# FNet and routed feed-forward on one core: w_r products read from PSUM, half columns of group two compared on GpSimd

## The chip, the core and the metric

The kernel runs on one core of one Trainium2 chip. The core has five engines with a queue each: TensorE (PE, with its weight loads as PEld), VectorE (DVE), ScalarE (ACT), GpSimd (POOL) and SyncE (SP). SP issues most of the loads, GpSimd issues the indirect loads and the stores. The metric is the device time of one execution in microseconds (us); several executions are timed and their median is given. A profiled execution has a time of its own, and a span: from the first to the last event that the profile shows.

## The reference, cut to what matters

A token sequence x of 2048 x 576 goes through two sublayers. The first normalises it and mixes it by two discrete Fourier transforms of which the real part is kept; the matrices of the transforms are inputs. The second scores each token with w_r, takes the one token with the highest score, runs a gated feed-forward of width 4608 on it, and adds the result to that row alone.

```python
xn = layernorm(x)
a, b = xn @ Wd_re.T, xn @ Wd_im.T
h = x + (Ws_re @ a - Ws_im @ b)
hn = layernorm(h)
r = hn @ w_r
i = argmax(r)                       # one token of 2048
y = (silu(hn[i] @ w_gate) * (hn[i] @ w_up)) @ w_down
out = h + hn                        # and, for row i alone:
out[i] += y * sigmoid(r[i])
```

## The kernel before, in words

The kernel uses symmetries that a matrix of such a transform has (columns that mirror one another, halves that repeat up to a sign), so that it computes with a quarter of each. It does not take them on trust: it loads the whole matrices, compares the parts that should mirror each other on VectorE (`off_s`, `off_t` and `off_h`, lines 375, 380 and 387), and ScalarE squares the differences and sums them up (`square`, line 368). If the sum of all squares is not nearly zero, a general path runs at the end in place of the short one; with these inputs it does not.

The 16 column blocks of the sequence matrices are folded into nine, which are worked on in two groups (`GROUPS`): blocks 1 to 5, and blocks 6, 7, 0 and 8. For each group PE runs the sequence transform (`seq`, line 565, five matmul groups numbered 0 to 4), ScalarE and VectorE bring its sums to Z (`keep`, lines 579 and 583), and PE runs the hidden transform block by block (`hid`, line 610). VectorE adds x to each result (`residual`, line 619) and multiplies the row with w_r and sums it up (`dot_h`, line 623); ScalarE takes the variance (`spread_of`, line 630). From these come the scores (`scores`, lines 639 to 642), in three batches, and the finished rows: 14 blocks on ScalarE (`result`, line 661), two on GpSimd (`result_on_pool`, line 654). GpSimd stores ten of the sixteen blocks (lines 676 and 678), SP the other six (`store_if`, line 1079), either early or as the last thing on its queue, by where the token lies.

The comparison by halves, `off_h`, takes one or two column blocks of a group and one of the two matrices (real, imaginary): two operations, one subtracts and one adds the two halves of 64 columns of every other piece. `c_half` plans them: two operations' worth for the real and two for the imaginary matrix, then one square over both. Group one has three such steps, group two has two (`HALVES`), with two column blocks each. The differences lie in Q, which has two slots; a slot is free again when ScalarE has squared it. The tiles D hold the matrices, D2 and D0 those of group two; once they have been used and compared, weights are loaded into them.

Then the token is found: VectorE takes the maximum of the scores over the columns, PE spreads it over the partitions (`spread`, line 255), VectorE picks row and column (`token`, `where`), ScalarE picks the token's row (`row_of_token`, line 1058), PE spreads it to all partitions (`to_all`, lines 1090 and 1091), VectorE normalises it into PSUM (`normalized`, line 1098), and ScalarE copies it to SBUF for GpSimd (`copy_xs`, line 1103).

The feed-forward runs over 36 rows of weights per partition in nine blocks of four. A block has a tile of w_gate, of w_up and of w_down, each loaded with 1152 KB (`load_ffn`, line 1200; two loads where the place is split, lines 1202 and 1208). There are 16 places for such tiles: in D, in the raw tiles R, in XF, W, Z and Q. The first 16 loads are issued as these come free, Q's last; the others follow when a tile's products are done. The down tiles of the last three blocks come behind all gate and up tiles. Products of gate and up rows with the token's row are taken by VectorE (line 1217, with the sum; line 1224, without) and by GpSimd (line 1228, 14 of them); ScalarE sums up what has no sum (line 1233). Per block ScalarE and VectorE form the gate (lines 1244 to 1247), and PE multiplies with the down tile (`down`, line 1255). Last, VectorE adds to the token's row (line 1268), and ScalarE's queue stores it (line 1278).

PSUM has eight banks. Four are used in pairs under the name y, four one by one under the name z: two for each `seq` group, two for each fold of an even block, and one each for the two spread keys (`pm`), the sum of errors (`pk`), the gate (`hs`), the output row (`pd`) and a matmul that only keeps PE busy (`spin`).

The order of each queue comes from a planner. `add` states an operation with its engine, an estimated duration and what it depends on; `order` computes for each the longest way to the end and then fills each engine's queue in time, taking of the operations that are ready the one with the longest way (`push` adds to it; the products with w_r have a push of -40, so that they come last among what is ready). The planner's times are estimates; at run time each queue runs in that order, and each operation waits for what it needs.

Of the kernel before, what the change touches and what calls it, by code (L numbers as in the profile page):

```python
# [7 lines left out]
F32 = mybir.dt.float32  # L8
# [3 lines left out]
OP = mybir.AluOpType  # L12
AX = mybir.AxisListType

P = 128
# [127 lines left out]
def kernel(  # L143
# [21 lines left out]

    def bank(name, tag, bufs):
        return psum.tile([P, 512], F32, tag=tag, name=name, bufs=bufs)

    def ypair(name):
# [4 lines left out]
    def ybank(name):  # L174
        return ypair(name)[0]

    def zbank(name):
        return bank(name, "z", 4)

# [62 lines left out]
    def newton(rs, sd, var, unit, scale, tag):  # L242
# [7 lines left out]
        dve.scalar_tensor_tensor(rs, u, 1.5 * scale, r0, op0=OP.add, op1=OP.mult)  # L250

    def spread(col, tag):

        pb = zbank(f"pm{tag}")
        pe.matmul(pb[:, :P], col.to_broadcast([P, P]), ident, start=True, stop=True)
        return pb[:, :P]
# [120 lines left out]
    def off_t(j, i, u):  # L377

        o = Q[:, u % 2, 14 * P : QW].rearrange("p (k m) -> p k m", m=P)
        dve.tensor_tensor(o, C[NK - j, i, False], C[j, i, False][:, :, ::-1], op=SIGN[i])  # L380

    def off_h(g, c, n, i, u):

        o = Q[:, u % 2, i * 9 * n * HM : (i + 1) * 9 * n * HM].rearrange("p (c k m) -> p c k m", k=9, m=HM)
        t = DT[g, i][:, c : c + n]
        for k, op in enumerate((OP.subtract, OP.add)):
            dve.tensor_tensor(o[:, :, k::2, :], t[:, :, k::2, 0:HM], t[:, :, k::2, HM:P], op=op)  # L387

# [141 lines left out]
    def fold(k):  # L530
        if k % 2:
            FO[k] = ypair(f"fo{k}")
        else:
            FO[k] = zbank(f"fe{k}"), zbank(f"fo{k}")
        for t, c, w in zip(FO[k], (1, 289), (288, 287)):
# [20 lines left out]
    def seq(g, n):  # L556

        w = len(GROUPS[g]) * HM
        ZP[g, n] = [zbank(f"ps{g}_{n}_{h}") for h in range(2)]
        parts = [(0, E0 + 2 * P, 64, 0), (1, O0 + 2 * P, 64, 64)]  # L560
# [60 lines left out]
    def dot_h(k):  # L621
        n = POS[k]
        dve.scalar_tensor_tensor(  # L623
            junk2, X[:, k, 0:D], 1.0, wr, op0=OP.mult, op1=OP.mult, accum_out=TD[:, n, 0:1]
        )

    def spread_of(k):
# [204 lines left out]
    def c_half(g, c, m):  # L832
        u, w = qs.take()
        cus = [[CU[j, i, False] for j in GROUPS[g][c : c + m]] for i in range(2)]
        n = [
            add("DVE", 0.16 + 0.62 * m, then(off_h, g, c, m, i, u), [d for _, d in cus[i]], w)
            for i in range(2)
        ]
        for i in range(2):
            for b, _ in cus[i]:  # L840
                users[b].append(n[i])
        squares(u, 9 * m * P, n)

    def squares(u, w, n, ps=P):
        SQUARES.append(add("ACT", 0.3 + w / 1200, then(square, u, w, ps), n))
        qs.users[u].append(SQUARES[-1])
# [76 lines left out]
    def hid_step(g, c):  # L923
# [14 lines left out]
        RES[j] = [add("ACT", 0.9, then(spread_of, k), r, push=EARLY[g]) for k, r in zip(ks, res)]  # L938
        DOT[j] = [add("DVE", 0.83, then(dot_h, k), r, ws, push=DOT_PUSH) for k, r in zip(ks, res)]
        for js in BATCHES:  # L940
            if j == js[-1]:
                batch(js)

# [81 lines left out]
    for c in range(len(GROUPS[1])):  # L1025
        hid_step(1, c)


# [92 lines left out]
    step = add("DVE", 1.0, where, slot, qx)  # L1121
    step = add("ACT", 2.0, row_of_token, step, slot, RESULTS)
    near = add("POOL", 1.0, other_rows, slot, push=50.0)
    step = add("PE", 1.2, to_all, step)
# [15 lines left out]
    def check_all():  # L1140
        T["pk"] = zbank("pk")
        pe.matmul(T["pk"][:, 0:1], ones, T["ok"][:, 0:1], start=True, stop=True)
# [94 lines left out]
    def gated(js, n):  # L1237
        if "hs" not in T:
            T["hs"] = zbank("hs")
            T["pd"] = zbank("pd")  # L1240
            dve.memset(T["pd"][0:97, :QD], 0.0)
# [18 lines left out]
    def keep_busy(w, j, n):  # L1260

        if "spin" not in T:
            T["spin"] = zbank("spin")
        for r in range(n):
# [266 lines left out]
```

## Time and profile before

| what | value |
|---|---|
| median of three runs | 197.7 us (197.67 to 199.01) |
| the profiled execution's own time | 199.04 us |
| its span | 197.4 us |
| busy: DVE, ACT, PE, POOL | 166.6, 140.4, 129.6, 117.2 us |
| moved by DMA | 77.81 MB, mean 394 GB/s |
| granted TensorE clock, mean | 0.865 |

An engine's busy time is a mean over stages with different limits. The page has the busy share in 40 slices of 4.9 us each; a digit is the share in tenths. In the timeline a row has the start and the length in us, the engine, the line, the operation and its tiles, and in brackets the idle time ahead of it and what ended it. In the list of groups stand the count, the busy time, the mean of one in ns, and the idle time ahead. A row of the windows has the stretch, its length, the busy time of PE, PEld, DVE, ACT and POOL with the number of instructions, the granted clock, the share of the DMA engines and GB/s; asked for one line of code, it shows only the engine of that line.

### The profile page before, as it was taken

What the parts mean: (1) busy time and instruction counts of PE and PEld (TensorE: products, weight loads), DVE (VectorE), ACT (ScalarE), POOL (GpSimd) and SP (SyncE); (2) the same over time, 40 slices, a digit from 0 to 9 for tenths busy, and PEclk for the clock granted to TensorE, in tenths of its full rate; (3) what the DMA queues carried; (4) which work ended last, traced back from release to release, by engine and by line L of the source; (5) the groups of instructions that cost most, each with busy time, mean ns of one, the idle gap of its engine ahead of it and who ended that gap; (6) DMA issues with size and microseconds to landing.
All of it is one profiled execution on the core that took longest, in us unless ns stands there. A gap on an engine that the chain in (4) does not pass through costs nothing. (4 is left out here: it accounts for less than half of the span.)

```text
span 197.4 us, 2794 instructions
## 1 busy us (share of the span) xinstructions
PE 129.6 (66%) x758; PEld 89.9 (46%) x758; DVE 166.6 (84%) x419; ACT 140.4 (71%) x259; POOL 117.2 (59%) x139
## 2 busy tenths in 40 slices
PE   0007999999999999799999986900232036263940
PEld 0005667754667788477876764700121013031430
DVE  4399996999899968999799999999947999989720
ACT  3198853684699578799389399889555999877630
POOL 6488888284637876359780000003874999999900
PEclk9999999999999999999999999975555555558797
DMA  5999999999899999999999999999999999999992
GB/s 171 408 418 412 413 409 406 411 381 330 281 405 411 411 363 402 400 410 411 416 405 414 418 424 420 426 422 412 424 431 425 420 428 424 422 431 414 412 427 99
DMA packets 14587, 77.81 MB, mean 394 GB/s; under 512 B 1951, under 2 KB 1955, under 8 KB 11239
## 3 DMA queue, kind: packets, MB, share of 16 engines
q1 hardware_dynamic: 10461, 56.56, 71.5%
q0 software_dynamic: 4096, 21.03, 26.5%
q8 instruction: 7, 0.11, 0.2%
q14 instruction: 13, 0.11, 0.1%
q10 hardware_dynamic: 10, 0.00, 0.0%
HBM read 72.86 MB, written 6.49 MB: 402 GB/s over the span
## 5 line engine op out<-in xcount | busy, mean ns | idle before, releaser
L368 ACT ACTIVATE Q<-Q 128x2944 bf16<-128x2944 bf16 (+5 forms) x26 | 55.4, 2132 | 18.5 <-DVE Q L380 8.9
L610 PE MATMUL py<-W,Z 128*128 128x289 f32 x180 | 45.4, 409 | 3.8 <-DVE X L619 3.8
L565 PE MATMUL ps<-D,XF 128*128 128x320 f32 (+3 forms) x216 | 45.0, 408 | 0.5 <-DVE Z L583 0.5
L301 POOL DMA_INDIRECT R<-in_ct_dram,ic x21 | 32.1, 1528 | 17.7 <-DVE Q L375 13.5
L610 PEld LDWEIGHTS py<-W,Z 128*128 128x128 f32 x180 | 33.6, 189 | 15.2 <-issue 4.5
L565 PEld LDWEIGHTS ps<-D,XF 128*128 128x128 f32 (+1 forms) x216 | 32.0, 172 | 13.0 <-issue 1.5
L1228 POOL TENSOR_TENSOR D<-D,Z 128x1152 f32<-128x1152 f32 x8 | 20.9, 2642 | 0.0
L676 POOL DMA_DIRECT2D out_dram<-X x1 | 0.6, 621 | 32.1 <-ACT X L661 32.1
L301 POOL DMA_INDIRECT D<-in_ct_dram,ic x11 | 13.8, 1250 | 7.6 <-DVE Q L380 4.6
L498 ACT ACTIVATE junk<-X,XT 128x576 bf16<-128x576 f32 x16 | 12.3, 771 | 7.8 <-DMA X<-in_x_dram 3.3
L1233 ACT ACTIVATE junk<-D 128x576 bf16<-128x576 f32 x20 | 13.7, 683 | 3.2 <-POOL D L1228 2.6
L1255 PE MATMUL pd<-XF,H 128*1 128x144 f32 x80 | 5.3, 439 | 14.6 <-DVE H L1247 11.3
L537 PE MATMUL fo<-W,diag 128*128 128x288 f32 (+1 forms) x8 | 4.2, 706 | 16.3 <-DVE diag L528 16.3
L375 DVE TENSOR_TENSOR Q<-R,D 128x896 bf16<-128x896 f32 x11 | 11.9, 1084 | 3.2 <-DMA D<-in_ct_dram 1.8
L387 DVE TENSOR_TENSOR Q<-D 128x640 bf16<-128x640 f32 (+3 forms) x20 | 12.8, 691 | 1.7 <-DMA W<-in_wt_dram 1.7
L380 DVE TENSOR_TENSOR Q<-R,D 128x1152 bf16<-128x1152 f32 x10 | 13.4, 1348 | 0.0
L630 ACT ACTIVATE junk<-X,TD 128x576 bf16<-128x576 f32 x16 | 12.3, 766 | 1.4 <-DVE X L619 1.3
L661 ACT ACTIVATE X<-X,BB,UP 128x576 f32<-128x576 f32 x14 | 10.8, 854 | 3.1 <-DVE BB L642 3.1
L623 DVE SCALAR_TENSOR_TENSOR junk<-X,wr 128x576 bf16<-128x576 f32 x16 | 12.1, 755 | 0.3
L375 DVE TENSOR_TENSOR Q<-D 128x896 bf16<-128x896 f32 x11 | 11.8, 1082 | 0.0
L619 DVE SCALAR_TENSOR_TENSOR X<-py,X 128x576 f32<-128x576 f32 x16 | 11.6, 748 | 0.0
L375 DVE TENSOR_TENSOR Q<-R 128x896 bf16<-128x896 f32 x10 | 10.7, 1082 | 0.1
(205 smaller groups left out, 260.8 us busy)
## 6 DMA issues: line engine op xcount, KB each, us to landing
D<-in_ct_dram SPq DMA_DIRECT2D x22, 576.0 KB
R<-in_ct_dram SPq DMA_DIRECT2D x10, 576.0 KB
D<-in_wu_dram SPq DMA_DIRECT2D x5, 1152.0 KB
D<-in_wd_dram SPq DMA_DIRECT2D x4, 1152.0 KB
R<-in_wg_dram SPq DMA_DIRECT2D x3, 1152.0 KB
D<-in_wg_dram SPq DMA_DIRECT2D x3, 1152.0 KB
out_dram<-X SPq DMA_DIRECT2D x2, 1440.0 KB
X<-in_x_dram SPq DMA_DIRECT2D x4, 576.0 KB
```

The source lines that it names most:

```text
L301: pool.indirect_dma_start(tile, None, view, bass.IndirectOffsetOnAxis(ap=rows, axis=0), element_offset=at)
L368: act.activation(t, t, AF.Square, accum_out=DS[0 : t.shape[0], n : n + 1])
L375: dve.tensor_tensor(o, C[j, i, True][:, 0:7, :], C[j, i, False][:, 7:0:-1, :], op=SIGN[i])
L380: dve.tensor_tensor(o, C[NK - j, i, False], C[j, i, False][:, :, ::-1], op=SIGN[i])
L387: dve.tensor_tensor(o[:, :, k::2, :], t[:, :, k::2, 0:HM], t[:, :, k::2, HM:P], op=op)
L498: act.activation(junk[:, 0:D], X[:, k, 0:D], AF.Square, bias=XT[:, n : n + 1], scale=-float(D), accum_out=VX[:, n : n + 1],)
L565: pe.matmul(cm(ZP[g, n][k % 2][p0 : p0 + m], w), XF[:, q, m0 : m0 + m], DT[g, i][:, :, k, 0:HM], start=k in (0, 1), stop=k in (6, 7),)
L610: pe.matmul(YP[GROUPS[g][c]][:, h, 0:w], Z[:, a, c * P : (c + 1) * P], w_block(a)[:, h * HD : h * HD + w], start=(a == 0), stop=(a == 4),)
L623: dve.scalar_tensor_tensor(junk2, X[:, k, 0:D], 1.0, wr, op0=OP.mult, op1=OP.mult, accum_out=TD[:, n, 0:1])
L630: act.activation(junk[:, 0:D], X[:, k, 0:D], AF.Square, bias=TD[:, n, 1:2], scale=-float(D), accum_out=VAR[:, n : n + 1],)
L1228: pool.tensor_tensor(t, t, xs.unsqueeze(1).to_broadcast([P, JW, D]), op=OP.mult)
L1233: act.activation(junk[:, 0:D], WB[w, j][:, r, :], AF.Copy, accum_out=acc[:, j + r : j + r + 1])
```

## The change

Three things are changed.

GpSimd takes the comparisons by halves of group two (`half_on_pool`), in the same order and with the same operands as VectorE had them. Their planned cost is 0.3 + 1.31 us per column block in place of 0.16 + 0.62.

The square of the last of these two steps is planned behind `row_of_token` (`HELD`, `behind`). So it runs on ScalarE after the token's row is picked. The sum of errors, and the load into Q, still wait for it.

The products with w_r read it from PSUM. `wr_again` copies it there once on ScalarE, into a pair of z banks, after the last `seq` group has taken its own; `dot_h` reads the halves of that pair. The dots are stated to the planner in `dots`, behind all steps of the hidden transform; each depends on its residual and on that copy, with the push of -40 as before. So that a pair can be had, the four z banks are now taken as two pairs (`zpair`): the folds of even blocks and the `seq` groups take a pair, as they took two banks; the two spread keys share one, `pk` and `spin` one, `hs` and `pd` one.

```diff
+    def zpair(name):
+
+        t = psum.tile([P, 2, 512], F32, tag="z", name=name, bufs=2)
+        return t[:, 0], t[:, 1]
+
     def zbank(name):
-        return bank(name, "z", 4)
+        return zpair(name)[0]
...
+    KEYS = []
+
     def spread(col, tag):
 
-        pb = zbank(f"pm{tag}")
+        if not KEYS:
+            KEYS.extend(zpair(f"pm{tag}"))
+        pb = KEYS.pop(0)
...
+    def half_on_pool(g, c, i):
+        return g == 1
+
     def off_h(g, c, n, i, u):
 
         o = Q[:, u % 2, i * 9 * n * HM : (i + 1) * 9 * n * HM].rearrange("p (c k m) -> p c k m", k=9, m=HM)
         t = DT[g, i][:, c : c + n]
         for k, op in enumerate((OP.subtract, OP.add)):
-            dve.tensor_tensor(o[:, :, k::2, :], t[:, :, k::2, 0:HM], t[:, :, k::2, HM:P], op=op)
+            eng = pool if half_on_pool(g, c, i) else dve
+            eng.tensor_tensor(o[:, :, k::2, :], t[:, :, k::2, 0:HM], t[:, :, k::2, HM:P], op=op)
...
-            FO[k] = zbank(f"fe{k}"), zbank(f"fo{k}")
+            FO[k] = zpair(f"fo{k}")
...
-        ZP[g, n] = [zbank(f"ps{g}_{n}_{h}") for h in range(2)]
+        ZP[g, n] = zpair(f"ps{g}_{n}")
...
         dve.scalar_tensor_tensor(
-            junk2, X[:, k, 0:D], 1.0, wr, op0=OP.mult, op1=OP.mult, accum_out=TD[:, n, 0:1]
+            halves_of(junk2), halves_of(X[:, k, 0:D]), 1.0, YP["w"], op0=OP.mult, op1=OP.mult,
+            accum_out=TD[:, n, 0:1],
         )
+
+    def wr_again():
+        t = psum.tile([P, 2, 512], F32, tag="z", name="wrz", bufs=2)
+        YP["w"] = t[:, :, 0:HD]
+        act.activation(YP["w"], halves_of(wr), AF.Copy)
...
         n = [
-            add("DVE", 0.16 + 0.62 * m, then(off_h, g, c, m, i, u), [d for _, d in cus[i]], w)
+            add(
+                *(("POOL", 0.3 + 1.31 * m) if half_on_pool(g, c, i) else ("DVE", 0.16 + 0.62 * m)),
+                then(off_h, g, c, m, i, u), [d for _, d in cus[i]], w,
+            )
             for i in range(2)
         ]
...
+        if (g, c + m) == (1, len(GROUPS[1])):
+            HELD.append((u, 9 * m * P, n))
+            return
         squares(u, 9 * m * P, n)
 
-    def squares(u, w, n, ps=P):
-        SQUARES.append(add("ACT", 0.3 + w / 1200, then(square, u, w, ps), n))
+    HELD = []
+
+    def squares(u, w, n, ps=P, behind=None):
+        SQUARES.append(add("ACT", 0.3 + w / 1200, then(square, u, w, ps), n, behind))
         qs.users[u].append(SQUARES[-1])
...
-        DOT[j] = [add("DVE", 0.83, then(dot_h, k), r, ws, push=DOT_PUSH) for k, r in zip(ks, res)]
-        for js in BATCHES:
-            if j == js[-1]:
-                batch(js)
+        NEW.append((j, ks, res))
+
+    NEW = []
+
+    def dots():
+        (z0, w0_), (z1, w1_) = zs.take(), zs.take()
+        wp = add("ACT", 0.7, wr_again, ws, w0_, w1_)
+        for j, ks, res in NEW:
+            DOT[j] = [add("DVE", 0.83, then(dot_h, k), r, wp, push=DOT_PUSH) for k, r in zip(ks, res)]
+            for js in BATCHES:
+                if j == js[-1]:
+                    batch(js)
...
     for c in range(len(GROUPS[1])):
         hid_step(1, c)
+    dots()
...
     step = add("ACT", 2.0, row_of_token, step, slot, RESULTS)
+    squares(*HELD[0], behind=step)
...
-        T["pk"] = zbank("pk")
+        T["pk"], T["spin"] = zpair("pk")
...
-            T["hs"] = zbank("hs")
-            T["pd"] = zbank("pd")
+            T["hs"], T["pd"] = zpair("pd")
```

More of the change, by code (lines that the diff above doesn't have):

```diff
@@ L164 @@
     ctx.enter_context(tc.manual_schedule())
-    def bank(name, tag, bufs):
-        return psum.tile([P, 512], F32, tag=tag, name=name, bufs=bufs)
     def ypair(name):
@@ L1260, in keep_busy @@
     def keep_busy(w, j, n):
-        if "spin" not in T:
-            T["spin"] = zbank("spin")
         for r in range(n):
```

## The prediction

> **What bounds the kernel now.** I read the page first, for the shares of the engines and the DMA rate slice by slice.
>
> ```profile
> span 197.4 us, 2794 instructions
> DVE  4399996999899968999799999999947999989720
> DMA  5999999999899999999999999999999999999992
> GB/s 171 408 418 412 413 409 406 411 381 330 281 405 411 411 363 402 400 410 411 416 405 414 418 424 420 426 422 412 424 431 425 420 428 424 422 431 414 412 427 99
> ...
> 40.00:57.00 17.00, 16.50 (x78) 9.97 (x78) 15.53 (x22) 11.65 (x17) 10.75 (x6) 1.00 0.98 338
> 155.06:198.00 42.94, 18.17 (x292) 9.30 (x292) 30.95 (x88) 28.57 (x81) 32.34 (x13) 0.66 0.91 379
> ```
>
> The first line is the span. The VectorE digits show the stretch on which the change works: full slices from 100 to 130 us. But the DMA digits are 9 in nearly every slice from the second to the last but one, and the rate stands at 400 to 430 GB/s except in slices 8 to 10 and 14. The windows view prices the first dip: 17 us at 338 GB/s where the neighbours have 412 cost 17 x (1 - 338/412) = 3.1 us. Behind 75 us no slice falls under 400. So from there on the transfers set the pace, and 77.81 MB have to move whatever the engines do.
>
> The second view is the end of the timeline, the third the DMA issues of SP's queue and their waits.
>
> ```profile
> 165.81 0.33 SPq L1200 DMA_DIRECT2D R<-in_wu_dram  x1
> L1079 SPq DMA_DIRECT2D out_dram<-X x2: 351/352/354, 173.8 to 176.6; - x2
> SPq L1079 <- DMA R<-in_wu_dram: 2.3, 1, 2.3
> ...
> 184.73 2.67 POOL L1228 TENSOR_TENSOR D<-D,Z 128x1152 f32<-128x1152 f32 x1
> 189.32 0.16 DVE L1247 TENSOR_TENSOR H<-hs,U 128x4 f32<-128x4 f32 x1
> 189.58 1.16 PE L1255 MATMUL pd<-D,H 128*1 128x144 f32 x32 [2.08 <-DVE H L1247]
> 190.56 1.16 PE L1255 MATMUL pd<-W,H 128*1 128x144 f32 x32
> 191.79 0.37 DVE L1268 SCALAR_TENSOR_TENSOR orow<-pd,sg,orow 97x144 f32<-97x144 f32 x1 [1.91 <-PE pd L1255]
> 192.30 1.12 ACTq L1278 DMA_DIRECT2D out_dram<-orow  x1
> ```
>
> The load of the w_up rows of block 28 was issued at 165.81. The late store on the same queue waited 2.3 us for it and was then issued at 176.6: the load took 10.8 us to land, so the queue was that deep. Five loads of 1152 KB (1.18 MB) follow it: gate and up of block 32, then down of blocks 24, 28 and 32. At the 0.42 MB per us of these slices (424 to 412 GB/s in the page's row) each takes 2.8 us: up of block 32 lands near 182.2, down of block 32 near 190.6. GpSimd took that up tile at 184.73, 2.5 us after it landed, and PE took the last down tile at 190.56, straight behind the one before, so it had landed by then, and not long before. From there 1.16 us of PE, 0.37 of VectorE and the store of the row at 192.30 lead to the end. Two chains meet here within some tenths of a us: the products that reach H at 189.32, and the last load near 190.4.
>
> The products' chain I followed back to the token:
>
> ```profile
> L1228 POOL TENSOR_TENSOR D<-D,Z 128x1152 f32<-128x1152 f32 x8 | 20.9, 2642 | 0.0
> ...
> 128.31 0.76 DVE L619 SCALAR_TENSOR_TENSOR X<-py,X 128x576 f32<-128x576 f32 x1
> 141.74 0.16 DVE L260 TENSOR_REDUCE gt<-R 128x1 f32<-128x16 f32 x1
> 145.95 0.96 ACT L1058 ACTIVATE diag<-X,ghp 128x288 f32 x2 [0.95 <-POOL near L1070]
> 150.37 0.65 ACT L1103 ACTIVATE Z<-xsp 128x576 f32<-128x576 f32 x1 [3.46 <-DVE sq L1134]
> 151.10 2.62 POOL L1228 TENSOR_TENSOR XF<-XF,Z 128x1152 f32<-128x1152 f32 x1 [2.91 <-ACT Z L1103]
> ```
>
> The 14 products that GpSimd takes (8 in the first row, 6 more on other tiles with 2.62 to 2.66 us) run back to back from 151.10 to 187.40: 36.3 us, with no idle time ahead of any but the first. They start when ScalarE has copied the normalised row (150.37), this when its row is picked (145.95), this when VectorE has all scores (141.74). And between the last residual (128.31) and the scores VectorE is busy with products with w_r. So the stretch that the change lightens is on the products' chain, but that chain shares the end with the loads.
>
> **The change part by part.** *The half columns.* Eight VectorE comparisons leave for GpSimd.
>
> ```profile
> 120.00:130.00 10.00, 5.60 (x8) 1.00 1.01 422
> L623 DVE SCALAR_TENSOR_TENSOR junk<-X,wr x16: 747/757/759, 116.1 to 139.9; 128x576 bf16<-128x576 f32 x16
> L1217 DVE SCALAR_TENSOR_TENSOR junk<-D,xsp 128x576 bf16<-128x576 f32 x12 | 9.0, 752 | 0.3
> ...
> 106.38 0.74 DVE L583 SCALAR_TENSOR_TENSOR Z<-ps,os 128x256 f32<-128x256 f32 x2
> 118.86 0.93 ACT L368 ACTIVATE Q<-Q 128x896 bf16<-128x896 bf16 x1
> 135.98 0.62 POOL L676 DMA_DIRECT2D out_dram<-X  x1 [32.10 <-ACT X L661]
> 121.72 0.33 SPq L1200 DMA_DIRECT2D D<-in_wd_dram  x1
> 133.50 0.33 SPq L1200 DMA_DIRECT2D Q<-in_wg_dram  x1
> 155.06 0.35 SPq L1200 DMA_DIRECT2D R<-in_wu_dram  x1
> 121.72:155.06 33.34, 9.19 (x30) 6.31 (x30) 28.65 (x100) 25.07 (x42) 14.05 (x22) 0.63 1.01 423
> ```
>
> The first row is the windows view of line 387 alone: 8 comparisons, 5.6 us of VectorE, four of 640 and four of 512 elements (2 columns x 5 or 4 pieces x 64). On GpSimd no half is in the trace. Nearest is the product of 1152 elements in 2642 ns, 2.29 ns an element: 640 and 512 elements give 1.47 and 1.17 us, 2.64 a pair and 10.6 us for four. The upper end is twice that, 21 us, because these read in runs of 64 and write bf16, which no GpSimd row has; the lower end is no slower than VectorE, 5.6 us. I take 10.6: same engine, same kind of operation, same count. They start when the slot of Q is free, that is behind ScalarE's square of 118.86 (0.93 us, and its sum read out by 119.9), on an engine that stood idle for 32 us ahead of 135.98: 119.9 + 5.3 = 125.2 for the first two columns (124.4 before), 130.5 for the last two (127.7 before). Behind them on GpSimd stand the stores, the two result rows and the token's tests, which began at 135.98: no later.
>
> Who waits for the halves? Loads into the tiles that they free, on SP's queue: the one at 121.72 would go at 122.6, the later ones by at most 2 us. The queue bears it. After 155.06 there moved 42.94 x 0.379 = 16.3 MB; 11 loads issued from then on are 13.0 and the six late rows 1.8, so 1.5 MB (3.6 us) were still queued at that time. From 121.72 to there moved 33.34 x 0.423 = 14.1 MB, while seven more loads (8.3 MB) and ten rows of stores (2.9 MB) were issued: 4.4 MB, or 3.2 without the load itself, lay queued at 121.72. That is 7.6 us of cover: 2 us later costs nothing, 8 us later would stop the DMA.
>
> *The products with w_r.* They read the row from PSUM. The rows above give a median of 757 ns for two SBUF operands, and 752 for one in PSUM at the same size: no price. [...] Added is one ScalarE copy of 576 elements, 0.65 us by the row at 150.37, in a stretch where ScalarE has gaps. It waits for the pair of banks of the last but one matmul group of group two, whose values VectorE takes at 106.4; the first of these products ran at 116.1. So that wait costs nothing unless the copy is issued over 9 us late.
>
> What the change of operand is worth is seen where a comparison of VectorE (two SBUF operands) ran beside GpSimd:
>
> ```profile
> 26.06 0.20 POOL L513 TENSOR_TENSOR BX<-MX,RX 128x4 f32<-128x4 f32 x1
> 30.63 1.27 POOL L513 TENSOR_TENSOR BX<-MX,RX 128x4 f32<-128x4 f32 x1
> 30.43 1.42 DVE L387 TENSOR_TENSOR Q<-D 128x640 bf16<-128x640 f32 x2
> ```
>
> The same GpSimd operation took 0.20 us, and 1.27 when it fell into the two comparisons from 30.43 to 31.85; it ended with them, and they took the 1.42 us that such a pair takes elsewhere. So GpSimd is held up by VectorE. Whether VectorE is held up by a longer GpSimd operation no row shows. [...] Behind 119.9 VectorE has no operation with two SBUF inputs left, once the halves are gone and w_r is in PSUM (residuals read PSUM too), but for the comparison at 119.23:
>
> ```profile
> 119.23 1.09 DVE L375 TENSOR_TENSOR Q<-D 128x896 bf16<-128x896 f32 x1
> 127.74 2.12 ACT L368 ACTIVATE Q<-Q 128x2304 bf16<-128x2304 bf16 x1 [0.38 <-DVE Q L387]
> 142.84 1.65 POOL L654 TENSOR_SCALAR X<-X,UP,BB 128x576 f32<-128x576 f32 x2
> ```
>
> It may lose nothing, or the rest of one half, up to 1.5 us. I put 1.1 us on that, the length of the comparison itself.
>
> *The last squares.* The square of the last two columns (2.12 + 0.19 us) leaves its place at 127.74 and runs behind the picking of the token's row. There ScalarE was idle for 3.46 us ahead of 150.37. 2.31 us fit into 3.46. The load into Q waits for it: issued at 133.50 before, near 143 now, with cover as above (4.4 MB at 121.72, plus six loads of 1.18 less 11.8 us x 0.423 MB: 6.5 MB were queued at 133.50, 15 us). The sum of errors needs it too, but only behind the normalised row.
>
> *The pairs of banks.* Same four banks, same users; the folds, keys and gate banks are only grouped otherwise. Nothing, while PE waits on no bank near the end.
>
> *Sum.* VectorE has 5.6 us less before 141.74 and 1.1 us goes to the ports: the token's row comes 4.5 us sooner, and its copy at 145.9. GpSimd's chain could end at 187.4 - 4.5 = 182.9, but the up tile of block 32 lands only at 182.2, so it ends near 184.9; its two sums (1.6 us) and the gate put H at 187.3. PE does blocks 24 and 28 by 189.6 and then waits for the last load, near 190.4, which nothing moves: 190.4 + 1.16 = 191.6 against 191.72. The end gains 0.1 to 0.5 us; I take 0.3. The span goes from 197.4 to 197.1. The profiled execution took 199.04 us, 1.6 more than its span; the runs' median is 197.7, so I forecast 197.4 for it, with 196.5 to 198.5 as this case's own range.
>
> **The rivals.** *Products' chain alone sets the end (faster).* If the last load landed well before 190, the whole 4.5 us would show: 193.2. For it speaks that PE shows no wait ahead of 190.56; against it the landing at 176.6 with five loads behind it. Chance 0.04.
>
> *GpSimd's halves are slow (slower).* At the upper end, 21 us, they end at 141. The square of the first two columns then blocks ScalarE's queue until 130.5, and the stores, the two result rows and the tests start at 141 in place of 136. The picking of the row needs the result rows: in the trace they lie 6.9 us behind the first store (135.98 to 142.84), 1.65 us long, so they would end near 149.5, and the row is picked 3 to 4 us later than at 145.95. The products' chain has no slack: 197.7 + 3 = 200.7. It decides from about 1.6 times my price on. For it speaks that a row with runs of 64 is missing; against it that the product of 1152 elements, with the same two operands, is the nearest row by far. Chance 0.11.
>
> *The plan's order shifts in the first 76 us.* The priorities come from the longest way to the end, and the comparisons' ways grow by the slower halves. The dip at 40 to 57 us holds 3.1 us that tiles of R and D came free too late. A better order gives back up to that, 2 us in the middle: 195.7, chance 0.07. A worse one takes as much: 199.7, chance 0.05. That the shift is about the same for all comparisons speaks against both.
>
> *It does not do what it says.* The products with w_r stay late in VectorE's order, which picks them last, and the time won is idle ahead of 128.31: the token's row comes when it did and the time stays at 197.7. Chance 0.05.
>
> **How the numbers follow.** The forecast has 0.68. A measurement of this kernel can tell about 1% (2 us) from no change. Within 1%: 0.68 + 0.05 = 0.73. Faster: 0.04 + 0.07 = 0.11. Slower: 0.11 + 0.05 = 0.16. The range from 195.5 to 199.9 holds the forecast, the unchanged case and both shifts of the order, 0.85; left out are the slow halves and the free chain, 0.15.
>
> **What would show it.** Right: eight GpSimd comparisons of 1.2 to 1.5 us between 119 and 132; no VectorE half of group two; the products with w_r at 750 ns, some of them ahead of 116; the normalised row's copy near 146; a square of 2304 elements between the row's pick and that copy; GpSimd's products with gaps, waiting for loads, and PE waiting for the last down tile near 190.4. Wrong: halves over 2.3 us each, a GpSimd store later than 136, SP's load into Q followed by a dip in the DMA rate, or a dip between 40 and 57 us that differs from 338 GB/s. The forecast fails if the rate behind 75 us is not what sets the end.

## The result, and the profile after

The changed kernel took 200.74 us in the median of five runs (199.67 to 205.24), the kernel before 197.70 us: a ratio of 1.010 with an interval of 1.006 to 1.014. Timed again, ten runs against 25, the unaltered kernel had a median of 199.73 against 198.39: 1.006 (1.002 to 1.010). The change costs some 0.6 to 1 per cent, 1.2 to 2 us. The forecast was 197.4 with a range to 199.9: the first median lies outside it, the second just inside.

The first profile of the changed kernel fell on a disturbed execution (205.24 us), so the one read here is that of the repeat, 198.82 us. Its page has these rows, to be laid beside those of before: the span, VectorE's busy tenths, the DMA tenths and the rate, slice by slice.

```profile
span 197.1 us, 2808 instructions
DVE  4399999989899699993999999999839999969550
DMA  5999999999999999999999999999999999999980
GB/s 182 421 416 408 411 411 406 417 390 331 400 413 404 413 379 404 410 410 407 409 411 415 425 424 419 421 420 416 427 426 423 416 415 419 424 428 418 414 365 20
```

The reader is to see two things. Behind the tenth slice nothing falls under 379 GB/s until the last two: the transfers still set the pace for most of the span. But in the last but one slice the rate is 365 in place of 427, and in the last 20 in place of 99. Before, transfers ran up to the end; now they are done and something else is late. The span of 197.1 us is no longer than the one shown of before (197.4), for this execution's early dip was shallower: 381 GB/s from 40 to 57 us where the other had 338. By the prediction's own sum the dip then costs 17 x (1 - 381/412) = 1.3 us in place of 3.1. What the transfers gained there, the end lost.

The timeline of the end shows where. The rows have start, length, engine, line, operation and, in brackets, the idle time ahead and what ended it; L1277 is the gate's sigmoid, L1279 its first product, L1288 the product with a down tile, L1299 the last operation on the token's row (L1244, L1246, L1255 and L1268 in the kernel before).

```profile
183.91 2.62 POOL L1262 TENSOR_TENSOR D<-D,Z 128x1152 f32<-128x1152 f32 x1
184.41 0.18 ACT L1277 ACTIVATE pd<-G 128x4 f32<-128x4 f32 x1 [1.36 <-PE pd L1288]
184.65 1.14 PE L1288 MATMUL pd<-XF,H 128*1 128x144 f32 x16 [0.36 <-ACT pd L1277]
185.92 0.17 DVE L1279 TENSOR_TENSOR pd<-pd,G 128x4 f32<-128x4 f32 x1 [2.17 <-PE pd L1288]
...
189.62 0.18 ACT L1277 ACTIVATE pd<-G 128x4 f32<-128x4 f32 x1 [1.48 <-PE pd L1288]
190.70 1.16 PE L1288 MATMUL pd<-W,H 128*1 128x144 f32 x32 [1.14 <-issue]
192.91 0.37 DVE L1299 SCALAR_TENSOR_TENSOR orow<-pd,sg,orow 97x144 f32<-97x144 f32 x1 [2.31 <-PE pd L1288]
193.42 1.12 ACTq L1309 DMA_DIRECT2D out_dram<-orow  x1
```

GpSimd begins its last product at 183.91, 0.8 us sooner than before (184.73). Yet the row's last operation comes at 192.91, 1.1 us later than before (191.79). The distance from the one to the other grew from 7.06 to 9.00 us. Inside it stand waits that the kernel before does not have: ScalarE waits 1.36 us and 1.48 us with a sigmoid for matmuls into `pd`, and VectorE waits 2.17 us with its product: not for the sigmoid, which is done at 184.59, but for the matmuls begun at 184.65. What stands behind it in VectorE's queue comes later with it. A gate does not need what PE adds up in `pd`; but in the changed kernel `hs`, where the gate is formed, and `pd`, where the row is summed, are the two banks of one pair.

Whether that is what ends last is told by the view of waits of SP's queue, because SP waits at the very end for every store. The columns are the engine and line, what was waited for, the sum, the number and the longest. First the kernel before, then the changed one.

```profile
SPq L1527 <- DMA out_dram<-X: 4.3, 2, 3.5
```

```profile
SPq L1558 <- DMA out_dram<-X: 4.3, 2, 3.4
SPq L1558 <- DMA out_dram<-orow: 2.4, 1, 2.4
```

Before, the stores of finished rows (`out_dram<-X`), which SP issues behind the last loads, landed last; the token's row had been stored by then, and SP did not wait for it. After the change the row lands 2.4 us behind them.

The stretch that the change lightens has these rows. L397 are the comparisons by halves, L250 to L252 and L655 to L656 the first batch of scores on VectorE, L1091 the picking of the row, L1136 the copy of the normalised row.

```profile
L397 POOL TENSOR_TENSOR Q<-D 128x640 bf16<-128x640 f32 (+1 forms) x8 | 11.1, 1430 | 17.5 <-ACT Q L374 17.5
L633 DVE SCALAR_TENSOR_TENSOR junk<-X,wrz 128x576 bf16<-128x576 f32 x16 | 12.0, 751 | 0.3
123.41 0.97 DVE L250 SCALAR_TENSOR_TENSOR uh<-VAR,r0h 128x6 f32<-128x6 f32 x1
124.41 1.46 DVE L251 SCALAR_TENSOR_TENSOR uh<-uh,r0h 128x6 f32<-128x6 f32 x1
125.90 1.19 DVE L252 SCALAR_TENSOR_TENSOR RS<-uh,r0h 128x6 f32<-128x6 f32 x1
127.01 1.57 DVE L655 SCALAR_TENSOR_TENSOR R<-TD,wsum 128x6 f32<-128x6 f32 x1
128.61 1.18 DVE L656 TENSOR_TENSOR R<-R,RS 128x6 f32<-128x6 f32 x1
140.25 0.17 DVE L656 TENSOR_TENSOR R<-R,RS 128x6 f32<-128x6 f32 x1
145.11 0.96 ACT L1091 ACTIVATE diag<-X,ghp 128x288 f32 x2 [1.18 <-POOL near L1102]
145.98 2.11 ACT L374 ACTIVATE Q<-Q 128x2304 bf16<-128x2304 bf16 x1
149.53 0.65 ACT L1136 ACTIVATE Z<-xsp 128x576 f32<-128x576 f32 x1 [1.36 <-DVE sq L1168]
```

Eight halves took 11.1 us on GpSimd, beside the 10.6 forecast. But five operations of six elements a partition took 0.97 to 1.57 us each beside them, where the last of them, L656, takes 0.17 once the halves are done (140.25). Together that is 6.37 us for what would be 5 x 0.17 = 0.85: 5.5 us of VectorE are gone again, as much as the halves had freed. The row is picked at 145.11, where the prediction had some 141.5 (145.95 less 4.5).

### The profile page after: what moved, and what is told of

Same layout as the page of the kernel before. It is cut to its first block, busy times and chain, and to the rows that moved or that the text cites. A ratio compares the mean times of both kernels' runs of the same rounds, so it can differ in the third digit from the quotient of the medians.

```text
span 203.5 us, 2808 instructions
## 1 busy us (share of the span) xinstructions
PE 131.5 (65%) x758; PEld 91.4 (45%) x758; DVE 166.9 (82%) x411; ACT 141.4 (69%) x260; POOL 138.0 (68%) x147
## 2 busy tenths in 40 slices
DMA packets 14588, 77.82 MB, mean 382 GB/s; under 512 B 1951, under 2 KB 1955, under 8 KB 11239
## 4 chain that ended last, share of the span: by engine, by line
DVE 25%; DMA 24%; issue 21%; POOL 20%; PE 6%; SPq 1%; ACT 0%; POOLq 0%; ACTq 0%; DVEq 0%
DMA D<-in_ct_dram 15%; POOL R L307 8%; DVE junk L633 5%; DMA D<-in_ct_dram,ic 5%; POOL D L307 5%; POOL D L1262 4%; DMA R<-in_ct_dram,ic 4%; PE pd L1288 3%; DVE Q L397 2%; DVE junk L1251 2%; DVE Q L381 2%; DVE X L629 2%; PE pk L1296 1%; POOL W L1262 1%; DVE R L1258 1%
## 5 line engine op out<-in xcount | busy, mean ns | idle before, releaser
L620 PE MATMUL py<-W,Z 128*128 128x289 f32 x180 | 46.8, 419 | 5.5 <-DVE Z L593 3.7
L307 POOL DMA_INDIRECT R<-in_ct_dram,ic x21 | 31.3, 1493 | 16.6 <-DVE Q L381 12.4
L620 PEld LDWEIGHTS py<-W,Z 128*128 128x128 f32 x180 | 34.8, 195 | 17.1 <-DVE Z L593 4.1
L575 PEld LDWEIGHTS ps<-D,XF 128*128 128x128 f32 (+1 forms) x216 | 32.9, 172 | 12.7 <-issue 2.5
L307 POOL DMA_INDIRECT D<-in_ct_dram,ic x11 | 19.7, 1794 | 5.5 <-issue 3.0
L397 POOL TENSOR_TENSOR Q<-D 128x640 bf16<-128x640 f32 (+1 forms) x8 | 11.1, 1431 | 12.9 <-ACT Q L374 12.9
L1267 ACT ACTIVATE junk<-D 128x576 bf16<-128x576 f32 x18 | 12.3, 682 | 2.0 <-POOL D L1262 1.3
L633 DVE SCALAR_TENSOR_TENSOR junk<-X,wrz 128x576 bf16<-128x576 f32 x16 | 12.0, 751 | 0.3
L1288 PE MATMUL pd<-XF,H 128*1 128x144 f32 x80 | 5.1, 406 | 10.1 <-DVE H L1280 6.1
L1251 DVE SCALAR_TENSOR_TENSOR junk<-D,xsp 128x576 bf16<-128x576 f32 x14 | 10.5, 752 | 0.4
```

The costliest lines, as they stand in the source:

```text
L307: pool.indirect_dma_start(tile, None, view, bass.IndirectOffsetOnAxis(ap=rows, axis=0), element_offset=at)
L397: eng.tensor_tensor(o[:, :, k::2, :], t[:, :, k::2, 0:HM], t[:, :, k::2, HM:P], op=op)
L575: pe.matmul(cm(ZP[g, n][k % 2][p0 : p0 + m], w), XF[:, q, m0 : m0 + m], DT[g, i][:, :, k, 0:HM], start=k in (0, 1), stop=k in (6, 7),)
L620: pe.matmul(YP[GROUPS[g][c]][:, h, 0:w], Z[:, a, c * P : (c + 1) * P], w_block(a)[:, h * HD : h * HD + w], start=(a == 0), stop=(a == 4),)
L633: dve.scalar_tensor_tensor(halves_of(junk2), halves_of(X[:, k, 0:D]), 1.0, YP["w"], op0=OP.mult, op1=OP.mult, accum_out=TD[:, n, 0:1],)
L1251: dve.scalar_tensor_tensor(halves_of(junk2[:, 0:D]), halves_of(WB[w, j][:, r, :]), 1.0, T["xs"], op0=OP.mult, op1=OP.mult, accum_out=acc[: ...
```

## The experiments

Four theories could make the end late. A: GpSimd's halves hold VectorE's small operations, so nothing is won and something lost. B: the late square, and so the late load into Q, leaves the DMA queue empty. C: the gathers of group two collide with a busier VectorE (in the first profile the rate fell to 255 GB/s beside them). D: the pair of gate and row. All ratios are against the kernel before, run beside on the same chip, and all but the last six kernels compute everything.

**The unaltered kernel and three edits.** First the changed kernel again:

> The changed kernel unaltered, for a profile of an undisturbed execution. Theory A (the shared ports): GpSimd's comparisons hold up the small VectorE operations of the first batch of scores, which have two SBUF inputs; five of them take 1.0 to 1.6 us each in place of 0.16 to 0.22, some 5 us in all, as much as VectorE was relieved of, and the token's row comes no sooner than before (copy at 150 to 152 us); time 199.7 to 201. Theory B (the held square): the load into Q, issued only behind that square near 149, blocks SP's queue, and the rate dips under 400 GB/s some 5 to 12 us later, for about 1 us in all. Theory C (the gathers): GpSimd's indirect loads between 90 and 110 us take over 3 us each beside a VectorE without gaps, and the rate falls to 255 to 370 GB/s there, as in the profile on record; queues are the same up to there in both kernels, so by C this dip comes in some executions of either kernel.

199.73 us, 1.0058 (1.0021 to 1.0095). The slices from 94 to 113 us hold 409 to 425 GB/s and the loss is still there, so C is out.

Then the halves back on VectorE, with all else kept:

```diff
     def half_on_pool(g, c, i):
-        return g == 1
+        return False
```

> Changed kernel with all half columns back on VectorE; the products with w_r in PSUM and the held square stay. A: the score arithmetic is fast again (0.16 to 0.22 us each), the token's row comes as before (copy near 150.4), and the time is that of before, 197.5 to 198.3. B: the time stays at 199 or more, since the load into Q still waits for the square. C: no difference to the changed kernel, about 200.

200.21 us, 1.0096 (1.0058 to 1.0134). With no half on GpSimd the loss is still there, so A does not cause it. The five operations of the first batch took 0.17 to 0.22 us again (129.50 to 130.41), so it is the halves on GpSimd that hold them. This run clears A, but it does not show the row as the last thing. In its profiled execution (span 198.2) SP waits at the end for the stores of X alone:

```profile
SPq L1558 <- DMA out_dram<-X: 4.7, 2, 3.9
```

Then the last square back in its old place:

```diff
-        if (g, c + m) == (1, len(GROUPS[1])):
-            HELD.append((u, 9 * m * P, n))
-            return
...
-    squares(*HELD[0], behind=step)
```

> Changed kernel with the last square in its old place; halves on GpSimd and the products with w_r in PSUM stay. A: the scores are still held up, the time stays near 200. B: the load into Q is issued before 140, the dip behind the token goes, and the time falls by about 1 us to 199 to 199.5. C: no difference.

200.58 us, 1.0102 (1.0032 to 1.0172). The load into Q went at 141.98 in place of 148.20, and nothing was gained: B is out. In its profile the row landed last again, 2.7 us behind the stores of X.

Then the scores' intermediates in PSUM, in free columns of the bank that holds w_r, so that each of the five operations has an operand outside SBUF (two small operations more a batch):

```diff
-        newton(rs, cols(SD, js), cols(VAR, js), UNIT, 1.0, f"h{js[0]}")
-        dve.scalar_tensor_tensor(r, tot, wsum[:, 1:2], dot, op0=OP.mult, op1=OP.add)
-        dve.tensor_mul(r, r, rs)
...
+        r0, t1, t2 = (YP["wt"][:, 1, at_ + 8 * q : at_ + 8 * q + n] for q in range(3))
...
+        dve.reciprocal(r0, cols(SD, js))
+        dve.scalar_tensor_tensor(u, var, EPS / UNIT, r0, op0=OP.add, op1=OP.mult)
+        dve.scalar_tensor_tensor(u, u, -0.5 * UNIT, r0, op0=OP.mult, op1=OP.mult)
+        dve.scalar_tensor_tensor(rs, u, 1.5, r0, op0=OP.add, op1=OP.mult)
+        dve.tensor_scalar(t1, tot, wsum[:, 1:2], None, op0=OP.mult)
+        dve.tensor_tensor(t1, t1, dot, op=OP.add)
+        dve.tensor_mul(r, t1, rs)
...
```

> Changed kernel in which the score arithmetic keeps its intermediate values in PSUM, so that none of its operations reads two tensors from SBUF (two small operations more per batch). Halves on GpSimd and the held square stay. A: the five slow operations take 0.16 to 0.25 us beside GpSimd's comparisons, the token's row comes 4 to 5 us sooner than in the changed kernel, and the time falls to 197 to 198. B: the square ends sooner too, so the load into Q comes earlier, and the dip is smaller; the time falls, but by 1 us at most. C: no difference, about 200.

198.59 us, 0.9988 (0.9945 to 1.0031). The timeline has the operations of that batch at their usual length again, save one:

```profile
124.46 0.16 DVE L662 SCALAR_TENSOR_TENSOR uh<-uh,wrz 128x6 f32<-128x6 f32 x1
125.11 0.17 DVE L665 TENSOR_TENSOR wrz<-wrz,TD 128x6 f32<-128x6 f32 x1
125.40 1.32 DVE L667 TENSOR_SCALAR UP<-RS 128x6 f32<-128x6 f32 x1
126.64 0.16 DVE L668 TENSOR_SCALAR wrz<-TD 128x6 f32<-128x6 f32 x1
```

The exception at 125.40 reads one tile in SBUF and writes one there, so an operation can be held without a second input. The row is picked at 143.59, 1.5 us sooner than in the unaltered kernel, where 4 to 5 were expected: the first batch took 2.87 us in place of 6.68, but the two later ones took 0.6 us more each with their added operations, and this execution reached the first batch 0.85 us later (124.04 against 123.19). The median is 1.1 us lower than that of the unaltered kernel. So A is real, and it takes back the lead that would have covered a late end; but e2 says that it does not make the end late.

**Theory D, both ways.** The gate goes with `pk`, the row shares with the bank that only keeps PE busy:

```diff
-        T["pk"], T["spin"] = zpair("pk")
+        T["pk"], T["hs"] = zpair("pk")
...
-            T["hs"], T["pd"] = zpair("pd")
+            T["pd"], T["spin"] = zpair("pd")
```

> Changed kernel with the gate and the output row in different pairs of banks: the gate shares one with the sum of errors, the row one with the matmul that keeps PE busy. Theory D (one tile): gate and output row in one tile make ScalarE's gate wait for PE's matmuls of the block before, and PE's matmuls for the gate, which stretches the end. D: no such wait is left, the last addition to the row comes 1 to 2 us sooner against the last GpSimd product, and the ratio to the kernel before falls from 1.006 to 0.998 to 1.002. A (the shared ports as the cause of the loss): the scores are as slow as before and the ratio stays at 1.005 to 1.01.

198.27 us against 198.62, 0.9985 (0.9952 to 1.0018). The end of its timeline:

```profile
184.53 2.65 POOL L1262 TENSOR_TENSOR D<-D,Z 128x1152 f32<-128x1152 f32 x1
188.71 0.16 ACT L1277 ACTIVATE pk<-G 128x4 f32<-128x4 f32 x1
191.57 0.37 DVE L1299 SCALAR_TENSOR_TENSOR orow<-pd,sg,orow 97x144 f32<-97x144 f32 x1 [1.91 <-PE pd L1288]
```

The sigmoid at 188.71 has no bracket: it waits for nothing that the trace shows. From the last product to the row it is 7.04 us, as before.

Now the other way, in the kernel before: only gate and row in one pair (it is taken from the y banks).

```diff
-            T["hs"] = zbank("hs")
-            T["pd"] = zbank("pd")
+            T["hs"], T["pd"] = ypair("pd")
```

> The kernel before with only this done to it: gate and output row share one tile of two banks (a y pair, free by then). D: the waits between gate and PE's matmuls appear, the ratio is 1.004 to 1.01. A: nothing changes, 0.998 to 1.002.

199.87 us, 1.0067 (1.0034 to 1.0099): this one edit makes the kernel before as slow as the changed one. The same waits appear (L1243 is the sigmoid there, L1245 its product), and the row lands last:

```profile
184.18 2.62 POOL L1228 TENSOR_TENSOR D<-D,Z 128x1152 f32<-128x1152 f32 x1
184.68 0.18 ACT L1243 ACTIVATE pd<-G 128x4 f32<-128x4 f32 x1 [1.36 <-PE pd L1254]
186.19 0.17 DVE L1245 TENSOR_TENSOR pd<-pd,G 128x4 f32<-128x4 f32 x1 [2.25 <-PE pd L1254]
189.78 0.18 ACT L1243 ACTIVATE pd<-G 128x4 f32<-128x4 f32 x1 [1.36 <-PE pd L1254]
193.06 0.37 DVE L1267 SCALAR_TENSOR_TENSOR orow<-pd,sg,orow 97x144 f32<-97x144 f32 x1 [2.31 <-PE pd L1254]
SPq L1526 <- DMA out_dram<-orow: 1.2, 1, 1.2
```

8.88 us from product to row. With the row apart, the halves on VectorE and the square in its old place, so that of the change only the products with w_r from PSUM are left:

> Control: of the change only the products with w_r in PSUM and the pairs of banks, with gate and row apart; halves on VectorE, the last square in its old place. D: as the kernel before, 0.998 to 1.002. If the copy of w_r, the products in PSUM or the other pairs cost anything: over 1.003.

198.06 us, 0.9994 (0.9960 to 1.0028): copy and products with w_r in PSUM cost nothing. And row apart with the scores' intermediates in PSUM:

> Changed kernel with gate and row apart and with the score arithmetic through PSUM. D and A together: the token's row is picked 2 us sooner than before and the end is free of the waits; the end is then set by the last load, as the prediction had it, so 0.994 to 0.999 of the kernel before. D alone: as in the run with the row apart, 0.998 to 1.002. A alone: as in the run with the scores through PSUM, 0.995 to 1.003.

198.73 us, 1.0014 (0.9986 to 1.0043). Its row is picked sooner (144.74 against 145.72 in f1), and nothing comes of it, where 0.994 to 0.999 was expected. In its profile PE waits for the last down tile (0.63 and less), and transfers run at 398 GB/s up to 194 us.

**What the operand in PSUM is worth.** The row apart (f1), and the products with w_r read it from SBUF again:

```diff
-            halves_of(junk2), halves_of(X[:, k, 0:D]), 1.0, YP["w"], op0=OP.mult, op1=OP.mult,
+            halves_of(junk2), halves_of(X[:, k, 0:D]), 1.0, halves_of(wr), op0=OP.mult, op1=OP.mult,
```

> The changed kernel with the row's bank apart from the gate's (f1), and the products with w_r read it from SBUF again; the halves stay on GpSimd. Shared ports, by operands: the products beside the halves then have two SBUF inputs and no PSUM one, so those between 118 and 131 us take up to 1.5 us each in place of 0.75, the halves are held in turn, and the token's row is picked 3 us or more behind f1's 145.7; the time is 1.005 to 1.02 of the kernel before. Rival (the PSUM operand is worth nothing, GpSimd holds only the small operations of the scores): the products keep to 0.75 us, the row is picked within 1 us of 145.7, and the time is 0.995 to 1.002.

199.17 us against 198.34, 1.0068 (1.0033 to 1.0104). The group of the halves, the rows of the products beside them, SP's issue of the load into Q and the windows view of 153 to 163 us:

```profile
L397 POOL TENSOR_TENSOR Q<-D 128x640 bf16<-128x640 f32 (+1 forms) x8 | 12.7, 1620 | 17.5 <-ACT Q L374 17.5
119.99 0.76 DVE L633 SCALAR_TENSOR_TENSOR junk<-X,wr 128x576 bf16<-128x576 f32 x1
120.79 1.70 DVE L633 SCALAR_TENSOR_TENSOR junk<-X,wr 128x576 bf16<-128x576 f32 x1
122.54 1.97 DVE L633 SCALAR_TENSOR_TENSOR junk<-X,wr 128x576 bf16<-128x576 f32 x1
149.67 0.33 SPq L1234 DMA_DIRECT2D Q<-in_wg_dram  x1
153.00:163.00 10.00, 2.10 (x32) 0.99 (x32) 9.68 (x25) 9.62 (x26) 10.00 (x5) 0.50 0.95 358
```

Two products took 1.70 and 1.97 us in place of 0.75, and the eight halves 12.69 us in place of 11.14: both sides are held. The row was picked at 146.57, 0.85 us behind f1, not 3. The load into Q, which waits for the square behind that, went at 149.67 (148.81 in f1), and the rate fell to 358 GB/s for 10 us (415 in f1): 10 x (1 - 358/415) = 1.4 us, about what the median lost. That it was this 0.86 us which emptied the queue was not tested by an edit of its own.

**What the end waits for.** With the row apart, a sooner row won nothing in f3. The next kernels load only the first of the four rows of the last down tile (0.29 MB in place of 1.18, 2.1 us less at 0.42 MB per us), and PE multiplies it four times. First the kernel before, cut so:

```diff
-            m = TW if (w, j) != FT[-1] else TW - 1
+            if (w, j) == FT[-1]:
+                sp.dma_start(t[:, 0:1], rows[:, j : j + 1, :])
...
-                    T["pd"][at(h), :QD], H[:, j : j + 1], WB["d", j0][:, r, h * QD : (h + 1) * QD],
+                    T["pd"][at(h), :QD], H[:, j : j + 1], WB["d", min(j0, NJ - TW)][:, r if j0 < NJ - TW else 0, h * QD : (h + 1) * QD],
```

> The kernel before, of whose last down tile only one of four rows is loaded (0.29 MB in place of 1.18, 2.1 us at 0.42 MB per us); PE multiplies that row four times, so the last three rows of w_down are left out of the result. Theory (the end is the later of the last load and the products' chain, which met in the kernel before): the chain stays, so the time falls by 0.2 us or nothing: 0.996 to 1.001. Rival one (the bytes alone set the end): 2.1 us less, 0.989. Rival two (neither, the load has long landed): 1.000, with the row's last operation at the same distance behind GpSimd's last product.

197.57 us, 0.9963 (0.9941 to 0.9985): 0.7 us of the 2.1. The two kernels beside it missed their edit:

> The changed kernel with the row's bank apart (f1) and the last down tile cut in the same way. Theory: its products' chain was at most 0.4 us ahead of that of the kernel before, so 0.994 to 0.999. Bytes alone: 2.4 us less than the kernel before, 0.988. Load long landed: as f1, 0.9985.

> The changed kernel with the row's bank apart and the scores' intermediates in PSUM (f3), and the last down tile cut in the same way. Here the token's row comes some 2 us sooner, and only the last load hid it. Theory: 0.987 to 0.993, PE without a wait for the last down tile, and the rest of the gain over f3 (about 2 us) shown. Bytes alone: 0.989 too, but then g2 and g3 fall as far. If something else sets the end: 0.998 to 1.002, as f3.

In these the planner puts the last down tile into two places, which another branch of `load_ffn` loads, and that one was not cut: both moved 77.82 MB. They are f1 and f3 again, but for PE's operand, and what was expected of the cut stayed untested. They gave 0.9992 (0.9948 to 1.0036) and 0.9980 (0.9950 to 1.0011). The second is of use all the same:

```profile
189.59 0.37 DVE L1313 SCALAR_TENSOR_TENSOR orow<-pd,sg,orow 97x144 f32<-97x144 f32 x1 [2.94 <-PE pd L1302]
SPq L1572 <- DMA out_dram<-X: 4.5, 2, 4.0
SPq L1572 <- DMA out_dram<-orow: 0.3, 1, 0.3
```

The row's last operation came 2.0 us sooner than in f1 (191.57), without a wait for the last load, and the time stayed. SP waited for the stores of finished rows, and the row, though stored 2 us sooner, landed only 0.3 us behind them. That points past the last load's own landing, the floor of the prediction, to the bytes queued behind it. The three kernels that follow make the cut in whichever place the tile lies:

```diff
+        if (w, j) == FT[-1]:
+            WB[w, j] = parts[0].rearrange("p (j d) -> p j d", j=JW)
+            sp.dma_start(WB[w, j][:, 0:1, :], rows[:, j : j + 1, :])
+            return
         if parts[0].offset + HALF == parts[1].offset:
...
```

The changed kernel with fewer bytes:

> The changed kernel, of whose last down tile one row of four is loaded (0.88 MB or 2.1 us at 0.42 MB per us are saved); PE multiplies that row four times, so the last three rows of w_down are left out of the result. Theory (the end is the later of two: the row's store, some 4.3 us behind the row's last operation, and the landing of the stores of X that are queued behind the last loads): the row is held by the shared bank, so next to nothing is gained over e1: 1.002 to 1.007. Bytes alone: 0.989 to 0.995. If neither sets the end: as e1.

200.33 us against 198.54, 1.0079 (1.0042 to 1.0117), a little above the 1.002 to 1.007 expected.

```profile
SPq L1562 <- DMA out_dram<-X: 4.0, 2, 3.3
SPq L1562 <- DMA out_dram<-orow: 4.3, 1, 4.3
```

2.1 us of transfers less and nothing won; the row now lands 4.3 us behind the stores (2.4 in e1). The row apart with fewer bytes:

> The changed kernel with the row's bank apart (f1), with the same 0.88 MB not loaded. Theory (the later of the two): the row's last operation stays near 191.6, so the span ends near 195.9 and the ratio is 0.994 to 0.998, as in g2. Bytes alone: 0.988. If bytes play no part: as f1, 0.9985.

197.56 us, 0.9932 (0.9896 to 0.9967), some 1 us less than f1 and a little more than expected; the row, at 191.58, is the later by 1.8 us.

```profile
191.58 0.37 DVE L1303 SCALAR_TENSOR_TENSOR orow<-pd,sg,orow 97x144 f32<-97x144 f32 x1 [1.91 <-PE pd L1292]
SPq L1562 <- DMA out_dram<-orow: 1.8, 1, 1.8
```

And the row apart, a sooner row and fewer bytes:

> The changed kernel with the row's bank apart and the scores' intermediates in PSUM (f3, g4), with the same 0.88 MB not loaded. Theory (the later of the two): the row's last operation is near 189.6 and the bytes end 2.1 us sooner, so the span ends near 194 and the ratio is 0.985 to 0.992, the only one of the three with the full gain. Bytes alone: 0.988 in all three. If bytes play no part: 0.998, as g4.

196.73 us, 0.9876 (0.9802 to 0.9951).

```profile
190.51 0.37 DVE L1312 SCALAR_TENSOR_TENSOR orow<-pd,sg,orow 97x144 f32<-97x144 f32 x1 [2.53 <-PE pd L1301]
SPq L1571 <- DMA out_dram<-X: 5.0, 2, 4.6
```

Here the stores are last again, though its row came at 190.51 and not at the 189.6 expected. Nothing, a part and all of it: bytes alone would have given the same gain three times, the row's chain alone none to h3 over g4. The end is the later of the two. Of the kernels that compute everything, none is faster than the one before beyond its interval.

## Why the prediction was wrong

*The pairs of banks: the step that failed.* The prediction said: "Same four banks, same users; the folds, keys and gate banks are only grouped otherwise. Nothing, while PE waits on no bank near the end." The users are the same, but who waits for whom goes by the pair. With gate and row in one, the last two sigmoids wait for matmuls into the row's bank and the next matmuls for the gate: 1.9 us more from the last product to the row. Undone (f1) the loss is gone; made alone (f2) it is there. I looked for waits that exist, and the step adds new ones between two tiles that had been apart. PE's own wait for the gate is short (0.36 us at 184.65); the long ones are those of ScalarE (1.36 and 1.48) and VectorE (2.17). With `pd` and `spin`, both written by PE, in a pair (f1), no such wait stands in the trace, and from the last product to the row it is 7.04 us.

*VectorE beside the halves: right in kind, five times too small.* "Behind 119.9 VectorE has no operation with two SBUF inputs left" is wrong: the scores of the first batch are such, five of them, and the 1.1 us set aside became 5.5. The direction that the trace of before could not show, VectorE held by GpSimd, is shown by the rows of e1 (0.97 to 1.57 us in place of 0.17 to 0.22). No run shows the 1.1 us that the sum gives "to the ports", nor any ports: the comparison for which it was set aside ran at 117.88 in e1 and took 1.08 us, as before (1.09), though its last 0.3 us fell beside the halves. This mis-sized term had little to do with the time as such, since the lead it took away ends at the bytes anyway (f3). Together with the pair it does count: in e1 the row is last by 2.4 us, and with a row 1.5 us sooner (e4) the ratio is 0.999.

*What bounds the kernel: right, one thing overlooked.* The transfers do set the pace, and a products' chain that ends sooner is hidden, as forecast: in g4 the row's last operation comes 2.0 us sooner than in f1, and the time stays. That the ratio of f1, 0.9985, is 0.3 us, the gain that the prediction named, is luck: its row was picked 0.2 us sooner than before (145.72 against 145.95) and not 4.5, and its interval holds no gain as well. But the prediction put the floor at the landing of the last down tile, 190.4, and what lands last are the 1.8 MB of stores behind it. I had counted them in the queue at 155 us and left them out at its end. So the row of the kernel before had some slack, which the pair's 1.9 us used up and passed. An estimate of it comes from g2: 2.1 us fewer transfers won 0.7, so the row stood some 0.7 us ahead of the stores. 1.9 less 0.7 is 1.2 us, beside the 1.2 that e1 and the 1.3 that f2 lost.

*The halves: right.* 11.1 us against 10.6, begun at 118.64 against 119.9. The loads that wait for them did not show in the rate (416 to 424 GB/s in the slices from 113 to 138 us of e1).

*The products with w_r: right.* A mean of 751 ns against 755, and 0.9994 for this part alone (f4). What the prediction put no number on is the gain: read from SBUF they are held like the scores (1.70 and 1.97 us, g1).

*The last square: right.* It ran from 145.98 for 2.11 us, and 1.36 us of ScalarE's gap were left. The load into Q went at 148.20 and not near 143, because the row was picked later; the 15 us of cover from 133.50 on just held (414 GB/s from 153 to 163 us), and at 149.67 (g1) they seem to have run out.

*The rivals.* None of the four came true. The chance of 0.16 for slower lay on slow halves and a worse order, neither of which was seen. That the slow halves' 200.7 meets the measured 200.74 is chance, for the halves took 11.1 us. VectorE's order is the old one up to 100.7 us (e1), far behind the first 76. The row came nearly when it did (145.11 against 145.95), as the fourth rival has it, but not by the order: the first product with w_r ran at 113.38, before at 116.08, and the operations held beside the halves took the lead back (5.5 us). The rate from 40 to 57 us differs by execution (338 in the profile of before, 377 in that of g2, which has the same program there), so it tells nothing of a planner's order.

*Open.* Why that early dip is deeper in some executions was not tried, nor whether the load into Q alone costs g1 its 1.4 us. Why e2, with gate and row in one pair, took longer in an execution in which the stores of X landed last is not shown either: its rate was 346 GB/s from 40 to 57 us and 383 from 57 to 76, where the profile of before has 338 and 397. That the pair costs the time rests on f1 and f2.

## What to carry to other kernels

When tiles are regrouped, list for each pair which engines write and read either half: here two users on different engines in one pair bought waits of 1.36 to 2.25 us for each other's work, though their banks differ, and the row came 1.8 us later behind the last product (f2). Before work is moved to GpSimd, list all that VectorE does meanwhile, small operations too: five with all operands in SBUF took 0.97 to 1.57 us here beside GpSimd comparisons of 1.27 to 1.73 (e1), in place of 0.17 to 0.22 (e2), and 5.5 us were lost where 5.6 had been moved. And follow the wait at the very end: here a chain ended 2.0 us sooner for nothing while stores were queued behind the last loads (g4).

## What was not expected of the hardware

VectorE operations of six elements a partition took 0.97 to 1.57 us beside GpSimd's comparisons (e1), six to nine times their 0.17 to 0.22 without them; with an input or the output in PSUM they kept 0.16 to 0.23 us (e4). For one of them a single input in SBUF was enough: `UP<-RS` took 1.32, while `uh<-uh,wrz`, with its other input in PSUM, took 0.16. Why, these runs don't show. Residuals and products with one operand in PSUM stayed at 0.75 (e1). With both operands in SBUF both sides lost: products of 0.75 us took up to 1.97, and eight halves 12.69 in place of 11.14 us (g1).
